# Pooled attention and a snake expert layer in f32: one more product of the hidden layer in the inner seven-product form, and the softmax one or two slots later

## The chip, the cores and the metric

One core of one Trainium2 chip runs the whole program. The metric is the device time of one execution in microseconds, as the median of several runs; before the change it is 899.29 us (three runs, 898.45 to 900.01). The profile is one execution of the same program with the hardware profiler on.

## The reference

Inputs q, k, v are f32 of shape (8, 8, 576, 64): batch, heads, sequence, head dimension. Keys and values are averaged over pools of 8 positions, so that each head has 72 keys. The result of the attention goes, head by head, into rows of 512 numbers and through two matrices with a snake activation in between:

```
k_p = k.reshape(B, H, 72, 8, D).mean(axis=3)          # v_p likewise
scores = scale * q @ k_p^T;  attn = softmax(scores)
x = (attn @ v_p) as (4608, 512)
h = x @ w_in                                          # 512 x 2048
s = sin(alpha * h)
g = h + s * s / (alpha + 1e-9)
out = g @ w_out                                       # 2048 x 512
```

All of it is in f32, and the output is (4608, 512).

## The kernel before

**Stages.** The first product (x @ w_in) runs in nine units of 512 rows, u = 0 to 8; the second (g @ w_out) follows in six units and takes the rest of the span. Between them g goes through a tensor in HBM (g_bridge). While unit u of the hidden layer runs, the attention of batch u+1 is worked out piece by piece beside it.

**The seven products.** Both matrix products use Winograd's form of Strassen's scheme: a product of 2x2 blocks is made of seven block products instead of eight, with sums of blocks before and after. In the hidden layer the outer scheme halves the rows (2 x 256), the 512 inputs (2 x 256) and the 2048 outputs (2 x 1024). The weights of product p are `self.A[p]`; the sums of x are `self.bt`. Each unit runs four groups J = 0 to 3 (`begin`, object `G`; `Q` is the group before), each with two blocks of 128 of the 1024 outputs in each half. Product p of a group is four matmuls of 128x128 weights on 256 columns (`product`, L866): two output blocks `jj`, two input blocks `kk`.

Some products of some groups are themselves made by the seven-product scheme (`inner_product`, L1058): instead of four matmuls of 256 columns, seven of 128 columns. Its steps are `a` (first and fifth inner product into the spare PSUM bank `y`, then two copies on ScalarE), `b` (sixth and second, one copy), `d` (seventh, one addition on VectorE, L1073) and `e` (third and fourth). The sums of weights come from `inner_w_in` (once, in unit 0, GpSimd), those of x from `inner_x` (in slot 2 of each unit, GpSimd, L823). Which groups do so stands in `I5` (outer product 5) and `I1` (outer product 1): in units 1 to 6 groups 2 and 3 for product 5, group 3 for product 1.

**Slots.** A group has seven slots, `k` = 0 to 6, one for each outer product in the order 1, 5, 6, 2, 7, 3, 4; slot = 7 J + k runs from 0 to 27. `hidden` writes down, slot by slot, what each engine does; engines run their own instructions strictly in that order and wait for each other by semaphores. The results of the seven products are combined in four PSUM banks of the group (`b1`, `b6`, `b5`, `b7`, out of five that rotate), by ScalarE copies (L839) from bank to bank onto which PE adds, and by VectorE additions (`add`, L838). Sines and squares are on ScalarE (`sin` L1028, `square` L1035); some of them belong to the group before and run a few slots late (`last_sines`, `squares`), as do the two additions that make g final (`finish`, L1080) and the stores to HBM (`store_g`, L1094).

**What is carried beside it.** `carry(u)` puts functions into slots (`at(slot, f)`; they run where `hidden` calls `extras()`, or ahead of the slot for halves such as 24.5). For batch u+1 in units 1 to 6: the scores in slots 3 and 5 (PE, L318) with their maxima and differences on VectorE (L341, L342); `exp` on ScalarE (L367; Exp is in another activation table than Sin, so that a table load stands before and after); `norm`: sum and reciprocal on VectorE (L373, L374), the quotient on GpSimd (L375); `turn`: 32x32 transposes of the attention on VectorE into the tile `tr` (L504 to L514); `move`: 16 DMAs on SyncE's queue that carry `tr` into `aM` (L524), each reading columns that all four `turn` write; `all_values` in slot 25: attention times values on PE (L613, L626), from `aM`. In slots 23 to 26 of units 0 to 5, `turn_q` (L229, L234, DMAs L244) transposes the queries of batch u+2; there is one tile `tr`, which it uses again. In the middle of it `finish_before` makes a part of `finish` that had been put off:

```
for e in range(2):
    x = main[:, 4 * e:4 * e + 4]...
    nc.vector.transpose(out=out, in_=x)
    if e == 0:
        self.finish_before()
```

That addition (L1080) reads bank `b7` of group 2, which `all_values` takes for its second set of products (`rest`). `load_k`, `load_v`, `pool_k`, `pool_v` bring the keys and values of coming batches (DMA on SyncE's queue) and sum them over pools (GpSimd, L132, L152).

Of the kernel before, what the change touches and what calls it, by code (L numbers as in the profile page):

```python
# [19 lines left out]
P = 128  # L20
# [20 lines left out]
class Kernel:  # L41
# [793 lines left out]
    def hidden(self, u, extra):  # L835
# [3 lines left out]
        copy = lambda o, x: nc.scalar.copy(out=o, in_=x)  # L839
        sin, square, early = self.sin, self.square, lambda G: G.J == (0 if G.u else 1)  # L840
        busy = 0 < u < self.B - 1
        I5, I1 = ((2, 3), (3,)) if busy else {7: ((2, 3), (2, 3)), 8: ((2, 3), (2, 3))}.get(u, ((), ()))
        split = lambda J: u == 0 and J == 2
        end = lambda J: u == 0 and J == 3

        def begin(J):
# [30 lines left out]
        for slot in range(7 * self.NJ):  # L877
            J, k = divmod(slot, 7)
            Q, G = self.before, self.group

            def extras():
                for f in extra[slot]:
                    f()
            for f in extra[slot - 0.5]:
                f()

            if k == 0:
                Q = self.before = G
                N = self.next
                G = self.group = N or begin(J)  # L890
                self.next = None
                if G.i5 and not N:
                    G.i5.a()
                if Q and not G.i5 and not end(J):
                    self.last_sines(Q, 2)
                extras()
                if G.i1:
                    G.i5.b()
                    self.last_sines(Q, 0)
                else:  # L900
                    product(G, 1, G.b1, True)
                    if G.i5:
                        product(Q, 4, Q.b7, part=(2, 3))
            elif k == 1:
                if not G.i1:
                    copy(G.b6[:], G.b1[:])
                if G.i5 and not G.i1:
                    self.last_sines(Q, 0)
                elif Q and not G.i1:
                    if end(J):  # L910
                        self.last_sines(Q, 2)
                    for i in (0,) if split(J) else (1, 0) if u == 0 else (0, 1):
                        squares(Q, i)
                extras()
                if not G.i5:
                    product(G, 5, G.b5, True)
            elif k == 2:
                if Q and not G.i5 and not split(J):
                    self.finish(Q)
                if not G.i1:  # L920
                    extras()
                if G.i1:
                    product(G, 6, G.b6, part=(0, 1))
                    G.i5.d()
                    self.last_sines(Q, 1)
                    square(Q, 1, 0)
                    self.late = Q
                    extras()
                    self.finish_before()
                    product(G, 6, G.b6, part=(2, 3))  # L930
                elif G.i5:
                    product(G, 6, G.b6, part=(0, 1))
                    G.i5.b()
                    self.last_sines(Q, 1)
                    squares(Q, 0)
                    product(G, 6, G.b6, part=(2, 3))
                else:
                    product(G, 6, G.b6)
            elif k == 3:
                late = J == 0 and busy  # L940
                if Q and not late and not G.i5 and not split(J):
                    self.store_g(Q)
                G.p5 = self.tp.tile([P, JW, TH], F32, name="p5")
                if G.i1:
                    if not busy:
                        copy(G.b7[:], G.b6[:])
                    square(Q, 1, 1)
                    squares(Q, 0)
                    extras()
                    product(G, 2, G.b1)  # L950
                    G.i5.e()
                    copy(G.p5[:], G.b5[:])
                else:
                    copy(G.b7[:], G.b6[:])
                    if G.i5:
                        squares(Q, 1)
                        G.i5.d()
                        self.finish(Q)
                        self.store_g(Q)
                    else:  # L960
                        copy(G.p5[:], G.b5[:])
                    if split(J):
                        squares(Q, 1)
                        self.finish(Q, (0,))
                    extras()
                    product(G, 2, G.b1)
            elif k == 4:
                if G.i1 and busy:
                    copy(G.b7[:], G.b6[:])
                    self.behind_order = lambda: sin(G, 0, 0, G.b1)  # L970
                else:
                    sin(G, 0, 0, G.b1)
                if not G.i5:
                    square(G, 0, 0)
                extras()
                if G.i1:
                    self.finish(Q, (1,))
                    self.store_g(Q)
                product(G, 7, G.b7, part=(0, 1))
                if G.i5:  # L980
                    if not G.i1:
                        G.i5.e()
                        copy(G.p5[:], G.b5[:])
                    square(G, 0, 0)
                product(G, 7, G.b7, part=(2, 3))
            elif k == 5:
                add(G.g[:, 1, :, 1], G.b7[:], G.p5[:])
                extras()
                if split(J):
                    self.finish(Q, (1,))  # L990
                    self.store_g(Q)
                N = None
                if J + 1 in I1:
                    N = self.next = begin(J + 1)
                    N.i1.a()
                product(G, 3, G.b6, part=(0, 1))
                if N:
                    N.i1.b()
                product(G, 3, G.b6, part=(2, 3))
            else:  # L1000
                if J == 0 and busy and Q:
                    self.store_g(Q)
                add(G.g[:, 0, :, 1], G.b6[:], G.p5[:])
                sin(G, 1, 1, G.g[:, 1, :, 1])
                N = self.next
                last = lambda: add(G.g[:, 0, :, 0], G.b1[:], G.s[:, 0, :, 0])
                if not N:
                    last()
                    extras()
                    product(G, 4, G.b7, part=(0, 1))  # L1010
                    if J + 1 not in I5 or J + 1 in I1:
                        product(G, 4, G.b7, part=(2, 3))
                else:
                    product(G, 4, G.b7, part=(0,))
                    N.i1.d()
                    last()
                    N.i5.a()
                    product(G, 4, G.b7, part=(1, 2))
                    N.i1.e()
                    copy(N.b6[:], N.b1[:])  # L1020
                    extras()
                    product(G, 4, G.b7, part=(3,))

    def sin(self, G, i, j, src):

        for jj in range(JW):
            f = i * self.K2 // 2 + G.J * JW + jj
            self.nc.scalar.activation(out=G.s[:, i, jj, j, :], in_=src[:, jj], func=AF.Sin, scale=self.al[:, f:f + 1])  # L1028
# [173 lines left out]
    def carry(self, u):  # L1202
# [6 lines left out]
        if u == 0:  # L1209
# [37 lines left out]
            at(19, A.move, (3,), nc.scalar)  # L1247
            at(26, A.all_values)
            at(9, self.load_q, 2)
            at(23, lambda: self.inner_w_in(((5, 2, 4), (1, 3, 4)), (lambda w: [w[:, i * 2 * P:i * 2 * P + 2 * P] for i in range(8)])(self.q_tile(0))))  # L1250
            for e in range(2):
                at(12, self.load_k, 2, e)
                at(17, lambda e=e: self.pool_k[e]())
# [5 lines left out]
        if 0 < u < last:  # L1259
            A = self.att[b]  # L1260
            for i in range(2):
                at((3, 5)[i], A.two_scores, i)
            at(6, A.two_shifts)
            for i in range(4):
                at((8, 9, 10, 10)[i], A.exp, i)
                at((9, 10, 11, 12)[i], A.norm, i)
                at((12, 13, 13, 13)[i], A.turn, i)
            at(14, A.move, range(4))
            at(6, self.load_v, b)
            at(12, lambda: self.pool_v())  # L1270
            for i in range(2):
                if b < last:
                    at(12, self.load_k, b + 1, i)
                    at(12, lambda i=i: self.pool_k[i]())
            at(25, A.all_values)
            if b < last:
                at(26, self.att[b + 1].k_t)
            if 2 < u + 2 <= last:
                at(7, self.load_q, u + 2)
            at(2, self.inner_x, u)  # L1280
            turn = 22
        elif u:
            turn = None
# [429 lines left out]
```

## Time and profile before

| | |
|---|---|
| median of three runs | 899.29 us (898.45 to 900.01) |
| span of the profiled execution | 896.2 us |
| hidden layer, units 0 to 8, L866 and L1058 | 19 to 513 us of the span |
| unit 2, as an example | 137 to 193 us, some 55 us each |
| L866 (256 columns) | 1808 matmul records |
| L1058 (128 columns) | 364 matmul records |
| out product, L1383 | 505 to 893 us |

How to read it. Every f32 matmul leaves two records, with two weight loads (PEld) beside them. A matmul's duration in the rows is longer than its step in the stream, since neighbours overlap; the distance from one start to the next is what it costs. A row of the timeline is: start in us from the span's beginning, length in us, engine, line, operation, out<-in, shapes, count, and in brackets the idle time of the engine before it with what ended it. Rows of one kind that follow each other are merged, and the length then runs from the first start to the last end. SPq are DMA issues on SyncE's queue; their length is the time of issuing, not of landing. In the tables by line the figures behind the bar are busy us, mean ns of one, and idle us before.

### The profile page before, as it was taken

How to read it: one execution, taken by the hardware profiler on the slowest of the kernel's cores; microseconds unless marked ns; L12 is line 12 of the kernel's file. 1: busy time of each engine (PE TensorE's matmuls, PEld its weight loads, DVE VectorE, ACT ScalarE, POOL GpSimd, SP SyncE). 2: the span in 40 equal slices, each digit the busy share in tenths (PEclk: the TensorE clock that was granted, in tenths of full speed). 3: DMA queues.
4: the chain of work that ended last, by engine and by line, in shares of the span. 5: the costliest groups of instructions: out<-in, count | busy, mean ns of one | idle time of the engine just before them, and what ended most of it. 6: DMA issues, size and time to landing. Idle time of an engine off the chain costs nothing.

```text
span 896.2 us, 16276 instructions
## 1 busy us (share of the span) xinstructions
PE 890.8 (99%) x6274; PEld 813.9 (91%) x6274; DVE 682.9 (76%) x918; ACT 438.6 (49%) x1033; POOL 249.2 (28%) x265
## 2 busy tenths in 40 slices
PE   9999999999999999999999999999999999999998
PEld 6787888888888888888888999999999999999998
DVE  7786857768577675765677889898897896996885
ACT  6687776877768777687776711111111211111111
POOL 6798443825338252434523000000000000000000
PEclk9999999999999999999999999999999999999999
DMA  9857957759586585648126243716435355164002
GB/s 269 244 158 206 244 147 212 187 164 254 139 214 186 183 225 147 175 140 302 53 106 219 102 181 103 232 37 218 117 105 160 89 159 159 37 192 142 20 18 53
DMA packets 119533, 141.03 MB, mean 157 GB/s; under 512 B 45776, under 2 KB 86496, under 8 KB 119456
## 3 DMA queue, kind: packets, MB, share of 16 engines
q1 hardware_dynamic: 116288, 137.39, 52.6%
q10 hardware_dynamic: 3168, 2.61, 1.0%
q8 instruction: 50, 0.82, 0.4%
q14 instruction: 27, 0.22, 0.1%
HBM read 75.37 MB, written 47.19 MB: 137 GB/s over the span
## 4 chain that ended last, share of the span: by engine, by line
PE 99%; DVE 0%; POOL 0%; ACT 0%; issue 0%; DVEq 0%
PE PS L866 44%; PE PS L1383 43%; PE PS L1058 5%; PE PS L318 2%; PE PS L613 2%; PE PS L626 1%; PE PS L1126 0%; PE PS L571 0%; PE PS L290 0%; PE PS L425 0%; PE PS L279 0%; PE PS L479 0%; PE PS L569 0%; POOL tr L451 0%; PE PS L403 0%; PE PS L487 0%
## 5 line engine op out<-in xcount | busy, mean ns | idle before, releaser
L866 PE MATMUL PS<-home,a 128*128 128x256 f32 x1072 | 253.0, 381 | 0.1
L866 PEld LDWEIGHTS PS<-home,a 128*128 128x128 f32 x1072 | 198.4, 190 | 30.9 <-issue 4.6
L866 PE MATMUL PS<-home,as 128*128 128x256 f32 x736 | 177.2, 382 | 0.0
L866 PEld LDWEIGHTS PS<-home,as 128*128 128x128 f32 x736 | 134.5, 190 | 18.1 <-ACT PS L839 1.2
L1383 PE MATMUL PS<-s,wb 128*128 128x192 f32 x672 | 116.2, 326 | 0.0
L1035 ACT ACTIVATE s<-s,c 128x256 f32<-128x256 f32 (+1 forms) x236 | 115.5, 556 | 0.0
L1383 PEld LDWEIGHTS PS<-s,wb 128*128 128x128 f32 x672 | 110.4, 190 | 0.1
L132 POOL TENSOR_TENSOR kvin<-kvin 96x768 f32<-96x768 f32 (+3 forms) x42 | 73.4, 1747 | 69.9 <-DMA kvin<-in_v_dram 67.8
L838 DVE TENSOR_TENSOR h<-PS,p 128x512 f32<-128x512 f32 x72 | 49.2, 684 | 55.5 <-PE PS L866 35.2
L1554 ACT COPY PS<-PS 128x192 f32<-128x192 f32 x42 | 12.7, 303 | 146.2 <-PE PS L1383 130.0
L1028 ACT ACTIVATE s<-h,al 128x256 f32<-128x256 f32 x144 | 65.5, 509 | 32.6 <-DVE h L838 32.6
L1383 PE MATMUL PS<-r,wb 128*128 128x192 f32 x432 | 79.0, 326 | 0.0
L1383 PEld LDWEIGHTS PS<-r,wb 128*128 128x128 f32 x432 | 71.6, 190 | 0.0
L1383 PE MATMUL PS<-s,a 128*128 128x192 f32 x384 | 70.2, 326 | 0.0
L1028 ACT ACTIVATE s<-PS,al 128x256 f32<-128x256 f32 x144 | 60.0, 469 | 17.2 <-PE PS L866 16.5
L1383 PEld LDWEIGHTS PS<-s,a 128*128 128x128 f32 x384 | 63.7, 190 | 0.0
L1080 DVE TENSOR_TENSOR h<-PS,s 128x512 f32<-128x512 f32 x36 | 24.8, 689 | 48.6 <-ACT s L1035 48.6
L839 ACT COPY PS<-PS 128x512 f32<-128x512 f32 x72 | 41.5, 577 | 34.5 <-PE PS L866 26.7
L1080 DVE TENSOR_TENSOR h<-h,s 128x1024 f32<-128x1024 f32 x36 | 55.3, 1537 | 3.3 <-ACT s L1035 3.1
L1584 ACT COPY PS<-PS 128x192 f32<-128x192 f32 x42 | 12.7, 303 | 89.5 <-PE PS L1383 89.5
L1322 DVE TENSOR_TENSOR s<-r 128x768 f32<-128x768 f32 x54 | 51.4, 951 | 4.8 <-PE PS L1383 2.8
L1383 PE MATMUL PS<-s,we 128*128 128x192 f32 x288 | 52.7, 326 | 0.0
(244 smaller groups left out, 1401.4 us busy)
## 6 DMA issues: line engine op xcount, KB each, us to landing
g_bridge<-h SPq DMA_DIRECT2D x72, 512.0 KB
r<-g_bridge SPq DMA_DIRECT2D x15, 1536.0 KB
x<-g_bridge SPq DMA_DIRECT2D x8, 1536.0 KB
out_dram<-o SPq DMA_DIRECT2D x90, 96.0 KB
kvin<-in_k_dram SPq DMA_DIRECT2D x14, 576.0 KB
q<-in_q_dram SPq DMA_DIRECT2D x7, 1024.0 KB
kvin<-in_v_dram SPq DMA_DIRECT2D x14, 512.0 KB
aM<-tr SPq DMA_DIRECT2D x54, 92.0 KB
```

What stands on the lines that cost most here:

```text
L132: self.nc.gpsimd.tensor_tensor(out=t[..., 0:w] if w > D else out, in0=t[..., 0:w], in1=t[..., w:2 * w], op=OP.add)
L318: nc.tensor.matmul(ps[e][r0 + r:r0 + r + q.shape[-1], h, :], q[s], kb[s, hp, :], start=True, stop=True)
L613: nc.tensor.matmul(o[r:r + 64], w, x, start=start and i < 2, stop=False, skip_group_check=True)
L838: add = lambda o, x, y: nc.vector.tensor_tensor(out=o, in0=x, in1=y, op=OP.add)
L839: copy = lambda o, x: nc.scalar.copy(out=o, in_=x)
L866: nc.tensor.matmul(ps[:, jj, :], self.A[p][:, kk, f * P:(f + 1) * P], x[:, kk, :], start=(start and n == 0), stop=(kk == 1), skip_group_ch ...
L1028: self.nc.scalar.activation(out=G.s[:, i, jj, j, :], in_=src[:, jj], func=AF.Sin, scale=self.al[:, f:f + 1])
L1035: self.nc.scalar.activation(out=x, in_=x, func=AF.Square, scale=self.c[:, f:f + 1])
L1058: nc.tensor.matmul(o, W[m][:, G.J - J0], X[m], start=start and n == 0, stop=True, skip_group_check=True)
L1080: add = lambda o, x, y: self.nc.vector.tensor_tensor(out=o, in0=x, in1=y, op=OP.add)
L1322: tt = lambda o, x, y, op: nc.vector.tensor_tensor(out=o, in0=x, in1=y, op=op)
L1383: nc.tensor.matmul(out, W[:, J // 2, J % 2, :], A[:, J, :], start=(start and J == 0), stop=(J == self.NJ - 1), skip_group_check=True)
```

## The change

In units 1 to 6, group 1 also makes its fifth product in the inner form: `I5` there goes from (2, 3) to (1, 2, 3), and the weight sums of product 5 are made for groups 1 to 3 instead of 2 and 3. `fast(G)` is true for that group, and its steps are placed by hand: `a` in slot 7, `b` in slot 8, `d` in slot 9, `e` in slot 10; half of the fourth product of group 0 goes from slot 6 to slot 8, some sines and squares are put to other slots, and `sin(G, 1, 1, ...)` of group 1 goes from slot 13 into slot 15. In `carry`, for units 1 to 6, `exp` goes from slots 8, 9, 10, 10 to 10, 10, 10.5, 10.5; `norm` from 9, 10, 11, 12 to 11, 11, 12, 13; `turn` from 12, 13, 13, 13 to 12, 13, 14, 14; `pool_v` and `pool_k` from 12 to 14. `move` stays in slot 14, `all_values` in 25, `turn_q` where it was.

```diff
-        I5, I1 = ((2, 3), (3,)) if busy else {7: ((2, 3), (2, 3)), 8: ((2, 3), (2, 3))}.get(u, ((), ()))
+        I5, I1 = ((1, 2, 3), (3,)) if busy else {7: ((2, 3), (2, 3)), 8: ((2, 3), (2, 3))}.get(u, ((), ()))
+        fast = lambda G: busy and G.J == 1
...
             if k == 0:
+                if fast(G):
+                    self.last_sines(Q, 0)
...
                     product(G, 1, G.b1, True)
-                    if G.i5:
+                    if G.i5 and not fast(G):
                         product(Q, 4, Q.b7, part=(2, 3))
             elif k == 1:
                 if not G.i1:
                     copy(G.b6[:], G.b1[:])
-                if G.i5 and not G.i1:
+                if fast(G):
+                    G.i5.b()
+                    product(Q, 4, Q.b7, part=(2, 3))
+                    self.last_sines(Q, 1)
+                    squares(Q, 1)
+                elif G.i5 and not G.i1:
+                    if fast(Q):
+                        sin(Q, 1, 1, Q.g[:, 1, :, 1])
                     self.last_sines(Q, 0)
...
             elif k == 2:
+                if fast(G):
+                    product(G, 6, G.b6, part=(0, 1))
+                    G.i5.d()
+                    self.finish(Q)
                 if not G.i1:
                     extras()
-                if G.i1:
+                if fast(G):
+                    product(G, 6, G.b6, part=(2, 3))
+                elif G.i1:
...
             elif k == 3:
-                    if G.i5:
+                    if fast(G):
+                        product(G, 2, G.b1, part=(0, 1))
+                        G.i5.e()
+                    elif G.i5:
...
                     extras()
-                    product(G, 2, G.b1)
+                    if fast(G):
+                        copy(G.p5[:], G.b5[:])
+                    product(G, 2, G.b1, part=(2, 3) if fast(G) else range(4))
             elif k == 4:
-                if not G.i5:
+                if not G.i5 or fast(G):
                     square(G, 0, 0)
                 extras()
...
-                if G.i5:
+                if G.i5 and not fast(G):
...
             else:
-                sin(G, 1, 1, G.g[:, 1, :, 1])
+                if not fast(G):
+                    sin(G, 1, 1, G.g[:, 1, :, 1])
...
-            at(23, lambda: self.inner_w_in(((5, 2, 4), (1, 3, 4)), (lambda w: [w[:, i * 2 * P:i * 2 * P + 2 * P] for i in range(8)])(self.q_tile(0))))
+            at(23, lambda: self.inner_w_in(((5, 1, 4), (1, 3, 4)), (lambda w: [w[:, i * 3 * P:i * 3 * P + 3 * P] for i in range(4)] + [w[:, 12 * P + i * P:13 * P + i * P] for i in range(4)])(self.q_tile(0))))
...
             for i in range(4):
-                at((8, 9, 10, 10)[i], A.exp, i)
-                at((9, 10, 11, 12)[i], A.norm, i)
-                at((12, 13, 13, 13)[i], A.turn, i)
+                at((10, 10, 10.5, 10.5)[i], A.exp, i)
+                at((11, 11, 12, 13)[i], A.norm, i)
+                at((12, 13, 14, 14)[i], A.turn, i)
             at(14, A.move, range(4))
             at(6, self.load_v, b)
-            at(12, lambda: self.pool_v())
+            at(14, lambda: self.pool_v())
             for i in range(2):
                 if b < last:
                     at(12, self.load_k, b + 1, i)
-                    at(12, lambda i=i: self.pool_k[i]())
+                    at(14, lambda i=i: self.pool_k[i]())
```

More of the change, by code (lines that the diff above doesn't have):

```diff
@@ L940, in hidden @@
                 late = J == 0 and busy
-                if Q and not late and not G.i5 and not split(J):
+                if Q and not late and (not G.i5 or fast(G)) and not split(J):
                     self.store_g(Q)
```

## The prediction

> **What bounds the kernel now.** I read the page first, then the waits, then unit 2 (137 to 193 us of the span) engine by engine in order of time.
>
> ```profile
> span 896.2 us, 16276 instructions
> PE 890.8 (99%) x6274; PEld 813.9 (91%) x6274; DVE 682.9 (76%) x918; ACT 438.6 (49%) x1033; POOL 249.2 (28%) x265
> PEclk9999999999999999999999999999999999999999
> PE 99%; DVE 0%; POOL 0%; ACT 0%; issue 0%; DVEq 0%
> ```
>
> PE is busy through the whole span at the full granted clock, and the chain that ended last is 99% PE. So the time is PE's own work plus every wait that PE is made to take; the other engines matter only where they make PE wait. The profiled execution spans 896.2 us, the median of the runs is 899.29, so 3.1 us lie around the span; I forecast on the span and add them back.
>
> **PE's work.** The rows below are the start of group 2 (J=2) of unit 2, which already has the seven-product form.
>
> ```profile
> 165.35 0.38 PE L1058 MATMUL PS<-home,as 128*128 128x128 f32 x2
> 165.79 2.76 PE L866 MATMUL PS<-home,a 128*128 128x256 f32 x12
> 168.39 1.09 PE L866 MATMUL PS<-home,as 128*128 128x256 f32 x4
> ```
>
> Each f32 matmul leaves two records. Two 128-column matmuls take 165.79-165.35 = 0.44 us; twelve records (six matmuls) of 256 columns take 168.39-165.79 = 2.60, or 0.433 each. The change takes four 256-column matmuls (1.73 us) out of group 1 in units 1 to 6 and puts in seven of 128 columns (7 x 0.22 = 1.54): 0.19 us less for each unit, 1.1 us in all. The wider sums of w_in are made once, on POOL in unit 0; one of before is
>
> ```profile
> 78.59 0.72 POOL L823 TENSOR_TENSOR q<-as,q 128x256 f32<-128x256 f32 x1
> ```
>
> and half as much again on four of them is about 1.4 us at 80 us of the span, long before group 1 of unit 1 (its moves start at 114.64, and group 1 some 16 us ahead of them, as 153.2 stands to 169.70 in unit 2 below). So I cost them at nothing; without that cover it would be 1.4 us, once.
>
> [...]
>
> **Where the other engines move.** With the fifth product in the new form, ACT gets three small copies more in group 1, and DVE one addition. The four exponentials go from slots 8 to 10 into slot 10 and the half slot after it, the quotients (DVE sum and reciprocal, POOL multiply) to slots 11, 11, 12, 13, the transposes (L504 to L514) to 12, 13, 14, 14. On DVE this gives the order: first two sums, first transpose, third sum, the two additions that close group 1 (L838), second transpose, fourth sum, third transpose, fourth transpose. Before, the fourth sum stood ahead of those last two additions. That matters, because the second of them waits for ACT's squares of s[0,0], and these now stand behind all exponentials and both table loads. The 16 moves of the transposed scores (L524, SP) wait for the end of the fourth transpose. I follow this chain through unit 2 with durations, or start-to-start distances, of before.
>
> ```profile
> 152.35 3.62 PE L866 MATMUL PS<-home,a 128*128 128x256 f32 x16
> 156.01 0.57 ACT L839 COPY PS<-PS 128x512 f32<-128x512 f32 x1 [0.30 <-PE PS L866]
> 156.49 1.33 ACT L1035 ACTIVATE s<-s,c 128x512 f32<-128x512 f32 x2
> 157.84 1.28 ACT L367 ACT_TABLE_LOAD   x1
> 159.13 1.26 ACT L367 ACTIVATE ex<-ex 128x576 f32<-128x576 f32 x2
> 160.30 0.58 ACT L839 COPY PS<-PS 128x512 f32<-128x512 f32 x1
> 161.29 1.49 ACT L367 ACTIVATE ex<-ex 128x576 f32<-128x576 f32 x2
> 162.80 1.28 ACT L1028 ACT_TABLE_LOAD   x1
> 164.10 0.84 ACT L1028 ACTIVATE s<-PS,al 128x256 f32<-128x256 f32 x2
> 164.82 0.90 ACT L1035 ACTIVATE s<-s,c 128x256 f32<-128x256 f32 x2
> ```
>
> PE begins the fourth product of group 0 at 152.35. After the change come half of it (0.87), the first inner pair (0.44), product 1 (1.73), the second inner pair (0.44) and the other half (0.87): 156.70. ACT has the result 0.20 later (PE passes to product 5 at 152.35+16 x 0.216 = 155.81, the copy starts at 156.01), so its sines of b7 start at 156.90. From there ACT runs without a gap: sines 0.72, squares 1.35, copy 0.48 (156.01 to 156.49), table load 1.29, two exponentials 1.17, copy 0.48, two exponentials 1.51, table load 1.30, sines 0.72, squares 0.90. That is 9.92, and the squares of s[0,0] end at 166.82, 1.1 us later than before (164.82+0.90 = 165.72).
>
> ```profile
> 164.39 1.02 DVE L373 TENSOR_REDUCE sm<-ex 128x12 f32<-128x876 f32 x1
> 165.44 0.23 DVE L374 RECIPROCAL sm<-sm 128x12 f32<-128x12 f32 x1
> 165.82 1.63 POOL L375 TENSOR_TENSOR ex<-ex,sm 128x864 f32<-128x864 f32 x1 [1.30 <-ACT s L1035]
> 166.13 0.68 DVE L838 TENSOR_TENSOR h<-PS,s 128x512 f32<-128x512 f32 x1
> 166.73 0.70 DVE L504 STREAM_TRANSPOSE tr<-ex 128x512 f32<-128x512 f32 x1
> 167.55 0.67 DVE L504 STREAM_TRANSPOSE tr<-ex 128x512 f32<-128x512 f32 x1
> 168.34 0.67 DVE L504 STREAM_TRANSPOSE tr<-ex 128x512 f32<-128x512 f32 x1
> 169.70 10.08 SPq L524 DMA_DIRECT2D aM<-tr  x16
> ```
>
> DVE's closing addition starts at 166.85 and takes 0.60; second transpose 0.82; fourth sum 1.05; from its reciprocal to POOL's multiply 0.38; the multiply 1.63: 171.33, with the third transpose beside it. Only then the fourth transpose, 1.36 from its start to the first move (168.34 to 169.70): 172.69. So **the moves start 3.0 us later than before**, in every one of the units 1 to 6.
>
> **Who waits for the moves.** SP issues them one behind the other, 10.08 us in unit 2, and nothing can hurry them. Two things stand behind the last one. PE's values (L613) read aM. And turn_q of the same unit (units 1 to 5) writes tr, the tile the moves read: its first transpose (L229) waits for all of them, and behind it on DVE stands the addition L1080 (finish_before), which frees the PSUM bank that PE's second group of value products writes.
>
> ```profile
> 65.52 7.88 SPq L524 DMA_DIRECT2D aM<-tr  x12
> 75.14 2.37 DVE L229 STREAM_TRANSPOSE tr<-q 128x1024 f32<-128x1024 f32 x2 [0.22 <-DMA aM<-tr]
> ...
> 114.64 11.20 SPq L524 DMA_DIRECT2D aM<-tr  x16
> 127.45 1.25 DVE L229 STREAM_TRANSPOSE tr<-q 128x1024 f32<-128x1024 f32 x1
> 128.62 0.65 DVE L1080 TENSOR_TENSOR h<-PS,s 128x512 f32<-128x512 f32 x1
> 129.85 0.65 PE L613 MATMUL PS<-aM,vm 64*64 64x512 f32 x6
> ```
>
> The first two rows are unit 0, where this wait already showed: L229 sat idle until the moves had landed, and started 1.74 us after SP was through with them (65.52+7.88 = 73.40). In unit 1 it started 1.61 us after SP's end (114.64+11.20 = 125.84), which bounds the landing from above there; I take 1.61. L1080 ends 1.82 us after L229's start, and PE can write 0.1 later. PE's second group stands 0.12 behind the first L613 row, at 129.97 in unit 1, where the addition frees the bank at 127.45+1.82+0.10 = 129.37. So before, 0.6 us were to spare in unit 1, and the moves now come 3.0 us late.
>
> ```profile
> 184.92 0.65 PE L613 MATMUL PS<-aM,vm 64*64 64x512 f32 x6
> 224.77 10.74 SPq L524 DMA_DIRECT2D aM<-tr  x16
> 239.98 0.65 PE L613 MATMUL PS<-aM,vm 64*64 64x512 f32 x6
> 280.17 10.08 SPq L524 DMA_DIRECT2D aM<-tr  x16
> 295.23 0.65 PE L613 MATMUL PS<-aM,vm 64*64 64x512 f32 x6
> 335.09 10.70 SPq L524 DMA_DIRECT2D aM<-tr  x16
> 350.30 0.65 PE L613 MATMUL PS<-aM,vm 64*64 64x512 f32 x6
> ```
>
> **The sum.** For each unit: end of SP's stretch + 3.0 + 1.61 + 1.82 + 0.10, against the first L613 row + 0.12.
> - unit 1: 125.84 + 6.53 = 132.37 against 129.97: +2.40
> - unit 2: 179.78 + 6.53 = 186.31 against 185.04: +1.27
> - unit 3: 235.51 + 6.53 = 242.04 against 240.10: +1.94
> - unit 4: 290.25 + 6.53 = 296.78 against 295.35: +1.43
> - unit 5: 345.79 + 6.53 = 352.32 against 350.42: +1.90
>
> Together +8.9. The shorter product is inside these figures (they compare ends, so PE just waits 0.19 longer). Unit 6 has no turn_q and keeps its gain, -0.2. Span 896.2+8.7 = 904.9, runs about **908.0 us**, 1.0% slower.
>
> Other terms stay near nothing. The copy of b6 after group 2's first product ends at about 168.15, PE wants it at 168.20; the addition inside the fifth product of group 2 stands behind the fourth transpose and comes just in time. Each can cost 0 to 0.2 us for a unit, but in units 1 to 5 what PE loses there it need not wait for later. POOL's sums of v and k are pushed back behind the last quotient, but only the values and the transposes of k after them want these. SP's next moves, those of q, start later too; the scores of the next unit want them, a whole stretch of moves later. Nothing excludes a small gain where a short wait of PE vanishes: I allow 0.3 us in all.
>
> **The rivals.**
> - *Only the gain* (not slower): no wait reaches PE, 899.29-1.1 = 898.2. It needs moves no more than about 0.4 us later than before in unit 1 (the 0.6 less PE's 0.19). For it: PE is the chain now. Against: the order on DVE, and L229 at its limit already.
> - *A shorter delay*: the squares finish early, or POOL's multiply hides. With the moves 2.0 us later each unit loses 1.0 less: 1.40+0.27+0.94+0.43+0.90-0.2 = 3.7, or 903.0.
> - *A longer tail*: the delay reaches 3.6 us, because instructions take longer beside new neighbours (no row shows that for these), 5 x 0.6 = 3.0 more: 911.
> - *The weight loads set the pace* for 128 columns:
>
> ```profile
> L1058 PEld LDWEIGHTS PS<-last,q 128*128 128x128 f32 x72 | 12.8, 191 | 1.2
> ```
>
>   at 0.19 us for each, one behind the other, fourteen of them are 2.7 us against 1.73, 5.6 us in all: 905 without any other wait. That two matmuls with their four loads go by in 0.44 us speaks against it: the loads overlap.
>
> **Chances.** The forecast 0.70, shorter delay 0.09, longer tail 0.08, only the gain 0.11, weight loads 0.02. What a measurement can tell from no change is about 0.2%, or 1.8 us: the gain alone is inside it. Faster by more than that needs gains that no row shows, 0.04 (out of the gain case); within it 0.08 (the other 0.07 of the gain case and 0.01 of the shorter delay); slower 0.88. The forecast's own range, with 0.4 us either way on the 3.0 (2 us over five units), is 905.5 to 910.5; to hold 8 in 10 I go from 903.0 to 911.0, which leaves out the gain case and half of the longer tail.
>
> **What would show it.** In the profile after: PE idle at the first L613 of units 1 to 5 with the moves or L1080 named; L229 idle until the moves landed, in all of them; moves first issued about 3 us later against group 2's first inner pair (4.35 us before: 165.35 to 169.70); group 1 shorter by 0.19 us. I am wrong if the fourth transpose ends within a microsecond of where it did, or if PE's rows show no gap ahead of L613.

## The result, and the profile after

The changed kernel takes 910.89 us (median of four runs, 909.31 to 911.99) against 899.65 us before (898.45 to 901.15) in the same series: the ratio is 1.0126, 95% interval 1.0113 to 1.0139. The forecast was 908.0, in a range of 903 to 911. The profiled run took 911.98 us, with a span of 910.2.

The page after: span, busy shares, and the chain of work that ended last by engine and by line.

```profile
span 910.2 us, 16372 instructions
PE 898.7 (99%) x6310; PEld 815.4 (90%) x6310; DVE 687.0 (75%) x924; ACT 442.3 (49%) x1051; POOL 249.4 (27%) x265
...
PE 89%; SPq 4%; ACT 2%; DVE 2%; DMA 1%; issue 1%; POOL 0%; DVEq 0%; ACTq 0%; POOLq 0%
PE PS L1405 42%; PE PS L867 36%; SPq L524 4%; PE PS L1080 3%; PE PS L318 2%; PE PS L613 2%; DMA aM<-tr 1%; ACT s L1057 1%; PE PS L626 1%; DVE h L1102 1%; DVE tr L229 1%; PE PS L1148 0%; ACT s L1050 0%; ACT PS L839 0%; DVE sm L445 0%
```

PE's busy share is 99% as before, so it doesn't show the loss; the chain does. Before, it was 99% PE. Now 4% of it are the moves' issues on SyncE (L524), followed by their landing, turn_q's transpose (L229) and the addition in finish_before. The changed kernel's lines are numbered a little differently: L866 is L867 now, and from L1028 on they stand 22 higher, so that L1035 is L1057, L1058 is L1080, and the addition L1080 is L1102. L229, L373, L504, L524, L613, L838 and L839 keep their numbers.

Unit 2 of the changed kernel in order of time (start, length, engine, line). The unit's first score matmul is at 147.48, against 144.15 before, so 3.33 us are to be taken off to stand beside the prediction's times. The row of before, and then the rows after:

```profile
144.15 1.33 PE L318 MATMUL PS<-kblk,q 64*64 64x72 f32 x64
```

```profile
147.48 0.54 PE L318 MATMUL PS<-kblk,q 64*64 64x72 f32 x15
168.91 2.76 PE L867 MATMUL PS<-home,a 128*128 128x256 f32 x12
169.25 0.90 ACT L1057 ACTIVATE s<-s,c 128x256 f32<-128x256 f32 x2
170.18 0.69 DVE L838 TENSOR_TENSOR h<-PS,s 128x512 f32<-128x512 f32 x1 [0.60 <-ACT s L1057]
170.96 0.57 ACT L839 COPY PS<-PS 128x512 f32<-128x512 f32 x1 [0.34 <-DVE h L838]
171.59 1.13 PE L867 MATMUL PS<-home,as 128*128 128x256 f32 x4
171.61 1.02 DVE L373 TENSOR_REDUCE sm<-ex 128x12 f32<-128x876 f32 x1
174.70 0.71 DVE L504 STREAM_TRANSPOSE tr<-ex 128x512 f32<-128x512 f32 x1 [1.05 <-POOL ex L375]
176.12 10.08 SPq L524 DMA_DIRECT2D aM<-tr  x16
188.12 1.25 DVE L229 STREAM_TRANSPOSE tr<-q 128x1024 f32<-128x1024 f32 x1 [2.46 <-DMA aM<-tr]
188.16 1.08 PE L613 MATMUL PS<-aM,vm 64*64 64x512 f32 x4
189.29 0.65 DVE L1102 TENSOR_TENSOR h<-PS,s 128x512 f32<-128x512 f32 x1
190.00 0.33 PE L613 MATMUL PS<-aM,vm 64*64 64x64 f32 x4 [0.76 <-DVE h L1102]
204.28 0.54 PE L318 MATMUL PS<-kblk,q 64*64 64x72 f32 x15
```

Read it downwards: the squares end at 170.15; the closing addition waited 0.60 us for them; only behind it come the fourth sum and, through POOL, the fourth transpose; the moves start at 176.12. At the other end L229 sat idle for 2.46 us until the moves had landed, the addition L1102 stands behind it, and PE waited for that addition. The row's 0.76 us is the smaller part of this wait, since the matmuls at 188.16 are drawn 1.08 us long: before, the second group of values began 0.12 behind the first, and here it begins 1.84 behind it (190.00 - 188.16). The 1.72 us between the two are what the unit lost (1.73, below). Counted from the unit's first score matmul, the moves start 28.64 us in (176.12 - 147.48), against 25.55 before (169.70 - 144.15): 3.09 us later.

The lengths of the units, from one first score matmul to the next, of the changed kernel's first profile and of a second one taken with the experiments:

| unit | before | after | more | forecast | second profile, more |
|---|---|---|---|---|---|
| 1 | 55.07 | 57.18 | 2.11 | 2.40 | 2.10 |
| 2 | 55.07 | 56.80 | 1.73 | 1.27 | 1.73 |
| 3 | 55.25 | 60.13 | 4.88 | 1.94 | 2.40 |
| 4 | 55.06 | 56.79 | 1.73 | 1.43 | 1.72 |
| 5 | 55.07 | 56.72 | 1.65 | 1.90 | 1.65 |

Unit 3 stands out in the first profile. From the timeline, its moves and the two rows in which PE waited:

```profile
232.92 11.79 SPq L524 DMA_DIRECT2D aM<-tr  x16
246.42 1.08 PE L613 MATMUL PS<-aM,vm 64*64 64x512 f32 x4 [1.38 <-DMA aM<-tr]
248.29 0.33 PE L613 MATMUL PS<-aM,vm 64*64 64x64 f32 x4 [0.79 <-DVE h L1102]
```

And the windows around them (window, its length, busy time and instructions of PE, PEld, DVE, ACT, POOL, granted clock, DMA share, GB/s):

```profile
244.00:249.00 5.00, 2.83 (x31) 1.68 (x33) 2.59 (x3) 2.15 (x5) 0.00 (x0) 1.00 0.79 265
249.00:253.00 4.00, 4.00 (x36) 1.54 (x28) 2.07 (x3) 0.90 (x3) 0.00 (x0) 0.57 0.28 66
253.00:257.00 4.00, 3.99 (x22) 2.98 (x19) 1.16 (x2) 3.57 (x12) 0.00 (x0) 1.00 0.53 127
```

The moves took SyncE 11.79 us there, 1.05 more than before in this unit, so PE waited twice, 1.38 and 0.79 us by the rows; behind that the mean granted clock of four microseconds was 0.57, which cost an estimated 4 x 0.43 = 1.7 us. Narrower windows show what the mean hides: the clock stood at 0.50 from 249.4 to 252.8, for 3.4 us, and at 1.0 on either side. In two of the four runs the mean clock was 0.998 (911.98 and 911.99 us), in the other two 1.0 (909.31 and 909.8).

### The profile page after: what moved, and what is told of

It reads as the page before. It is cut to its first block, busy times and chain, and to the rows that moved or that the text cites. A ratio compares the mean times of both kernels' runs of the same rounds, so it can differ in the third digit from the quotient of the medians.

```text
span 910.2 us, 16372 instructions
## 1 busy us (share of the span) xinstructions
PE 898.7 (99%) x6310; PEld 815.4 (90%) x6310; DVE 687.0 (75%) x924; ACT 442.3 (49%) x1051; POOL 249.4 (27%) x265
## 4 chain that ended last, share of the span: by engine, by line
PE 89%; SPq 4%; ACT 2%; DVE 2%; DMA 1%; issue 1%; POOL 0%; DVEq 0%; ACTq 0%; POOLq 0%
PE PS L1405 42%; PE PS L867 36%; SPq L524 4%; PE PS L1080 3%; PE PS L318 2%; PE PS L613 2%; DMA aM<-tr 1%; ACT s L1057 1%; PE PS L626 1%; DVE h L1102 1%; DVE tr L229 1%; PE PS L1148 0%; ACT s L1050 0%; ACT PS L839 0%; DVE sm L445 0%
## 5 line engine op out<-in xcount | busy, mean ns | idle before, releaser
L867 PE MATMUL PS<-home,a 128*128 128x256 f32 x1072 | 255.9, 381 | 0.1
L867 PEld LDWEIGHTS PS<-home,a 128*128 128x128 f32 x1072 | 197.5, 190 | 29.8 <-issue 4.9
L867 PE MATMUL PS<-home,as 128*128 128x256 f32 x688 | 168.1, 383 | 0.0
L867 PEld LDWEIGHTS PS<-home,as 128*128 128x128 f32 x688 | 125.0, 190 | 17.1 <-ACT PS L839 1.8
L1057 ACT ACTIVATE s<-s,c 128x256 f32<-128x256 f32 (+1 forms) x236 | 115.5, 556 | 0.0
L132 POOL TENSOR_TENSOR kvin<-kvin 96x768 f32<-96x768 f32 (+3 forms) x42 | 71.2, 1695 | 69.8 <-DMA kvin<-in_v_dram 68.1
L838 DVE TENSOR_TENSOR h<-PS,p 128x512 f32<-128x512 f32 x72 | 49.4, 686 | 53.5 <-PE PS L867 34.4
L1102 DVE TENSOR_TENSOR h<-h,s 128x1024 f32<-128x1024 f32 x36 | 55.9, 1552 | 3.3 <-ACT s L1057 3.1
L839 ACT COPY PS<-PS 128x512 f32<-128x512 f32 x72 | 41.7, 579 | 30.5 <-PE PS L867 20.9
L1405 PEld LDWEIGHTS PS<-s,we 128*128 128x128 f32 x288 | 47.8, 190 | 0.1
```

The source lines that it names most:

```text
L132: self.nc.gpsimd.tensor_tensor(out=t[..., 0:w] if w > D else out, in0=t[..., 0:w], in1=t[..., w:2 * w], op=OP.add)
L838: add = lambda o, x, y: nc.vector.tensor_tensor(out=o, in0=x, in1=y, op=OP.add)
L867: nc.tensor.matmul(ps[:, jj, :], self.A[p][:, kk, f * P:(f + 1) * P], x[:, kk, :], start=(start and n == 0), stop=(kk == 1), skip_group_ch ...
L1057: self.nc.scalar.activation(out=x, in_=x, func=AF.Square, scale=self.c[:, f:f + 1])
L1102: add = lambda o, x, y: self.nc.vector.tensor_tensor(out=o, in0=x, in1=y, op=OP.add)
L1405: nc.tensor.matmul(out, W[:, J // 2, J % 2, :], A[:, J, :], start=(start and J == 0), stop=(J == self.NJ - 1), skip_group_check=True)
```

## The experiments

**The two halves of the change, each alone.** First the later slots without the new product:

```diff
 (before)
-                at((8, 9, 10, 10)[i], A.exp, i)
-                at((9, 10, 11, 12)[i], A.norm, i)
-                at((12, 13, 13, 13)[i], A.turn, i)
+                at((10, 10, 10.5, 10.5)[i], A.exp, i)
+                at((11, 11, 12, 13)[i], A.norm, i)
+                at((12, 13, 14, 14)[i], A.turn, i)
...
-            at(12, lambda: self.pool_v())
+            at(14, lambda: self.pool_v())
...
```

> The kernel before with the later slots alone: exponentials, quotients, transposes and the sums of v and k where the changed kernel has them, the fifth product of group 1 in its old form (16 matmuls of 256 columns). Theory (the late fourth transpose makes the loss, whatever the product's form): the squares of s[0,0] stand behind the four exponentials again, end about 1.5 us later than before, the fourth sum behind the closing additions; the moves start 3.0 to 3.6 us later than before, PE waits ahead of L613 in units 1 to 5 as in the changed kernel, and the gain of 0.19 us a unit is missing. Beside it the copy of b6 that PE's second product of group 2 wants comes later, up to 0.9 us a unit. 899.6 + 11 to 12.5 = 911 to 912. Rival (the inner form itself is what costs, through its small copies and additions, and the later slots are hidden): no wait ahead of L613, 899.6 as before.

Measured: 914.37 us, ratio 1.017 (1.0155 to 1.0186). The later slots alone lose all that the change loses, and more. From the views of one line, what L613 waited for (idle us of its engine, times, over the whole run):

```profile
  DVE h L1080: 3.0, 5
  DMA aM<-tr: 0.9, 1
```

and L866:

```profile
  DVE h L838: 3.2, 6
```

The waits are those of the changed kernel, at the same place, and beside them the one for the copy of b6, once in each of the units 1 to 6. The time passed the expected 912 by 2.4 us: the moves start 3.75 us later than before against the unit's start (177.71 in unit 2, which begins at 148.41), a little more than the 3.0 to 3.6 expected, and SyncE took 11.71 us for them in unit 3. The rival, that the inner form itself costs, is out as the cause of these waits.

Then the new product with the old slots:

```diff
 (after)
-                at((10, 10, 10.5, 10.5)[i], A.exp, i)
-                at((11, 11, 12, 13)[i], A.norm, i)
-                at((12, 13, 14, 14)[i], A.turn, i)
+                at((8, 9, 10, 10)[i], A.exp, i)
+                at((9, 10, 11, 12)[i], A.norm, i)
+                at((12, 13, 13, 13)[i], A.turn, i)
...
-            at(14, lambda: self.pool_v())
+            at(12, lambda: self.pool_v())
...
```

> The changed kernel with the slots of before for the exponentials, quotients, transposes and sums of v and k; the fifth product of group 1 in the inner form. Theory: moves start no more than about 0.8 us later against the unit's start than before, so no wait ahead of L613; but two exponentials now stand ahead of the copy of b7 on ACT, and PE waits about 1.2 us a unit for that copy at the seventh product of group 1: 899.6 - 1.1 + 6 x 1.2 = about 905.5, with PE's wait inside group 1 and not at L613. Rival 1 (the form brings only its gain): 898.5. Rival 2 (the inner form itself makes the late moves): waits at L613 as in the changed kernel, about 911.

Measured: 905.92 us, ratio 1.0074 (1.0059 to 1.0089). L613 waited for nothing in units 1 to 6; L867 waited for ScalarE, and unit 2 shows where:

```profile
161.36 1.28 ACT L367 ACT_TABLE_LOAD   x1
162.65 1.26 ACT L367 ACTIVATE ex<-ex 128x576 f32<-128x576 f32 x2
163.82 0.58 ACT L839 COPY PS<-PS 128x512 f32<-128x512 f32 x1
164.45 1.35 PE L867 MATMUL PS<-home,a 128*128 128x256 f32 x5 [1.08 <-ACT PS L839]
173.28 10.07 SPq L524 DMA_DIRECT2D aM<-tr  x16
```

The copy of b7 stands behind a table load and two exponentials, and PE's seventh product waits for it. So the old slots do not suit the new product: with them it costs 1.2 us a unit at another place. The moves start 1.2 us late here (26.75 us into the unit, where at most 0.8 was expected), but PE comes 1.1 us later to its values too (41.90 against 40.77 us into the unit), and nobody waits for them.

**Where the delay comes from.** The changed kernel with the fourth quotient back ahead of the closing additions:

```diff
 (after)
-                at((11, 11, 12, 13)[i], A.norm, i)
-                at((12, 13, 14, 14)[i], A.turn, i)
+                at((11, 11, 12, 12)[i], A.norm, i)
+                at((13, 13, 14, 14)[i], A.turn, i)
```

> The changed kernel with the fourth quotient one slot earlier (slots 11, 11, 12, 12; transposes 13, 13, 14, 14), so that the fourth sum stands ahead of the closing additions of group 1 on DVE, as before the change; everything else as in the changed kernel. Theory (the closing addition, late through ACT's squares, ahead of the fourth sum is what makes the moves 3.0 us late): the moves start about 1.6 us later than before instead of 3.1, PE's waits ahead of L613 shrink to about 1.0 in unit 1, 0.6 in units 3 and 5, 0.1 in unit 4: 901.2 (900.5 to 903). Rival (the later exponentials alone make the moves late, the order on DVE does not matter): moves 3 us late as before, 910.9.

Measured: 900.83 us, ratio 1.0024 (1.0014 to 1.0034). Unit 2 in its timeline:

```profile
166.47 1.02 DVE L373 TENSOR_REDUCE sm<-ex 128x12 f32<-128x876 f32 x1
168.50 0.69 DVE L838 TENSOR_TENSOR h<-PS,s 128x512 f32<-128x512 f32 x1 [0.20 <-ACT s L1057]
171.50 0.67 DVE L504 STREAM_TRANSPOSE tr<-ex 128x512 f32<-128x512 f32 x1
172.87 10.07 SPq L524 DMA_DIRECT2D aM<-tr  x16
```

The sum stands 2.0 us ahead of the closing addition instead of 1.4 behind it, the moves start 1.53 us late instead of 3.09, and four fifths of the loss are gone (0.0024 of 0.0126). The exponentials are as late as in the changed kernel, so their lateness alone doesn't make it. The reverse, the same reordering in the kernel before:

```diff
 (before)
-                at((9, 10, 11, 12)[i], A.norm, i)
-                at((12, 13, 13, 13)[i], A.turn, i)
+                at((9, 10, 11, 13)[i], A.norm, i)
+                at((12, 13, 14, 14)[i], A.turn, i)
...
-            at(12, lambda: self.pool_v())
+            at(14, lambda: self.pool_v())
...
```

> The kernel before with the fourth quotient alone one slot later (slots 9, 10, 11, 13; transposes 12, 13, 14, 14; the sums of v and k at slot 14): no inner form in group 1, exponentials in their old slots. The fourth sum stands behind the closing additions of group 1. Theory: the moves start about 2.4 us later than before and PE waits ahead of or inside L613 by 1.8 in unit 1, 0.7 in unit 2, 1.3 in unit 3, 0.8 in unit 4, 1.3 in unit 5: 898.6 + 5.9 = 904.5 (903 to 906.5). Rival (only later exponentials make the wait, by way of ACT): 898.6.

Measured: 903.4 us, ratio 1.0058 (1.0043 to 1.0073). In unit 2, which begins at 145.67:

```profile
173.21 10.08 SPq L524 DMA_DIRECT2D aM<-tr  x16
```

The moves start 1.99 us late, 0.4 less than expected, and the time is 1.1 below the forecast. This reordering, with neither the new product nor a later exponential, costs 4.9 us. It also carries the sums of v and k from slot 12 to 14; these stand at 14 in the run with the earlier quotient too, where four fifths of the loss are gone, so they aren't what costs.

**How the delay reaches PE.** The changed kernel with finish_before called first:

```diff
 (after, turn_q)
-                nc.vector.transpose(out=out, in_=x)
                 if e == 0:
                     self.finish_before()
+                nc.vector.transpose(out=out, in_=x)
```

> The changed kernel with finish_before called ahead of the first transpose of turn_q, so that the addition that frees PE's bank no longer stands behind a transpose that waits for the moves. Theory (the wait runs moves, then turn_q's transpose, then that addition, then PE): PE waits only for the moves' own landing. From the landings in the changed kernel that is about 0.9 us in unit 1, 0.5 in unit 3, 0.4 in unit 5 and near 0 else; with the gain of 1.1 and small stalls at the sixth product of group 2 the sum is 901 (900 to 903). Rival (PE waits for the moves themselves, the addition is beside the point): 910.9, no change.

Measured: 901.38 us, ratio 1.0026 (1.0017 to 1.0036). Unit 2, and unit 3, where the moves are slowest to issue; the transpose is L231 here:

```profile
174.56 10.08 SPq L524 DMA_DIRECT2D aM<-tr  x16
185.21 0.69 DVE L1102 TENSOR_TENSOR h<-PS,s 128x512 f32<-128x512 f32 x1 [1.11 <-ACT s L1057]
186.56 2.37 DVE L231 STREAM_TRANSPOSE tr<-q 128x1024 f32<-128x1024 f32 x2 [0.66 <-DMA aM<-tr]
186.60 0.65 PE L613 MATMUL PS<-aM,vm 64*64 64x512 f32 x6
...
229.58 11.35 SPq L524 DMA_DIRECT2D aM<-tr  x16
```

The moves start 28.64 us into the unit, exactly as late as in the changed kernel, yet four fifths of the loss are gone here too (0.0026 of 0.0126 is left). The transpose still waits for the landing, but the addition is done before it, and PE goes on. What is left are waits for the landing itself, ahead of the first values: 0.92 us in unit 1 and 1.10 in unit 3, as the distance from one matmul's start to the next beyond the usual step of 0.22. So the wait ran through the addition behind the transpose.

**Both repairs.** The two diffs above together.

> The changed kernel with both repairs: the fourth quotient one slot earlier (slots 11, 11, 12, 12; transposes 13, 13, 14, 14) and finish_before called ahead of turn_q's first transpose. Theory: the moves start 1.5 us later than before, land about 1 us ahead of PE in every unit, and nothing on DVE that PE wants stands behind them; no wait ahead of or inside L613 is left. Of the inner form's gain of 1.1 us the stall at the sixth product of group 2 (about 0.1 us a unit more than before) takes 0.5: 898.0 against 898.6 of the kernel before, between 897.3 and 898.8. Rival (the two repairs take away the same wait, so that the second adds nothing): 900.8 as with the earlier quotient alone.

Measured: 898.78 us, ratio 1.0003 (0.9991 to 1.0014): no difference from before can be told. The chain of its page is PE's again:

```profile
PE 97%; DMA 2%; SPq 0%; issue 0%; POOL 0%; DVE 0%; POOLq 0%
```

and the timeline of unit 2 shows where the gain of the new product went:

```profile
146.60 0.60 PE L318 MATMUL PS<-kblk,q 64*64 64x72 f32 x19
167.59 0.38 PE L1080 MATMUL PS<-home,as 128*128 128x128 f32 x2
168.03 2.76 PE L867 MATMUL PS<-home,a 128*128 128x256 f32 x12
171.67 0.38 PE L1080 MATMUL PS<-last,q 128*128 128x128 f32 x2
```

Group 2 begins 20.99 us into the unit (167.59 - 146.60) against 21.20 before (165.35 - 144.15): the gain of about 0.2 us is real. But from the twelve records of 256 columns to the next inner pair it takes 171.67 - 168.03 = 3.64 us, where the kernel before took 169.31 - 165.79 = 3.52, up to this row:

```profile
169.31 0.39 PE L1058 MATMUL PS<-last,q 128*128 128x128 f32 x2
```

PE waits there for the copy of b6, which waits for the closing addition, which waits for the squares. Of 0.21 us a unit 0.12 are given back at once, and unit 4 of this profile lost another 0.3 (55.38 us long against 55.06), for a cause that wasn't followed. The repairs took away different waits, so the second did add something; but there was little left to win.

**What a longer wait does to the clock.** The changed kernel once more, and a dose:

> The changed kernel once more, for its unit 3, which lost 4.9 us in the first profile where the other units lost about 1.7 to 2.1. Theory (unit 3's moves take SP 0.7 to 1.7 us longer than those of units 2 and 4 every time, so PE waits longer there, and after that wait the granted clock falls for some us): unit 3 again loses 3 us or more, with the clock under 0.7 behind the first L613. Rival (the clock fell by chance): unit 3 loses about 2.5 us, with the clock at 1.0, and the span is 1.5 to 2 us shorter. The median stays at 910.9 either way within 1.5.

Measured: 911.69 us, ratio 1.0147 (1.0129 to 1.0164). The profiled execution had no fall: unit 3 is 57.65 us long, 2.4 more than before, at a clock of 1.0, with moves of 10.96 us; its span is 907.2. The other three runs had mean clocks of 0.998, 0.998 and 0.995, at 911.66, 911.73 and 914.02 us; the profiled one, at 1.0, 908.97. So the fall isn't bound to unit 3 of every run. That it comes by chance isn't shown by this: PE's waits at the values of unit 3 were shorter here, 0.56 and 0.79 us instead of 1.38 and 0.79, since the moves took less long.

```diff
 (after)
-                at((12, 13, 14, 14)[i], A.turn, i)
-            at(14, A.move, range(4))
+                at((12, 13, 14, 18)[i], A.turn, i)
+            at(18, A.move, range(4))
...
-            at(14, lambda: self.pool_v())
+            at(18, lambda: self.pool_v())
...
```

> The changed kernel with the fourth transpose, the moves and the sums of v and k at slot 18 in place of 14, behind three additions of DVE (L1095 and both L1102 of group 2's fifth product), which end at 179.76 in unit 2 of the changed kernel's profile. A dose, to see what a longer wait of PE does to the granted clock, which fell to 0.57 for about 4 us behind the 2 us of waits in unit 3 of the changed kernel, and stayed at 1.0 behind the waits of 0.7 to 1.4 us of the other units. The transposes run from 179.8, the moves start at 181.2 in place of 176.1, 5.1 us later, and PE waits as much longer in units 1 to 6: 911 + 6 x 5.1 = 941.5 (936 to 944) by the waits alone, mean clock 1.0 or 0.999. Theory (a wait of 2 us or more lowers the clock behind it each time): a stretch at 0.5 to 0.7 behind L613 in each of the six units, 4 x 0.43 = 1.7 us more for each, about 951, mean clock near 0.99. Rival (the falls come by chance, not with the wait): none or one such stretch, 941 to 944.

Measured: 954.04 us, ratio 1.0617 (1.0592 to 1.0642), mean clock 0.977 to 0.98. PE's wait in unit 2, from the timeline:

```profile
187.88 10.68 SPq L524 DMA_DIRECT2D aM<-tr  x16
200.26 2.44 PE L613 MATMUL PS<-aM,vm 64*64 64x512 f32 x8 [3.96 <-DMA aM<-tr]
```

and windows of 6 us around the first values of units 2, 3 and 6 (the clock is the third figure from the end):

```profile
200.00:206.00 6.00, 5.74 (x48) 2.72 (x48) 4.66 (x5) 0.90 (x3) 0.00 (x0) 0.50 0.14 32
265.00:271.00 6.00, 5.59 (x48) 2.72 (x48) 4.66 (x5) 0.90 (x3) 0.00 (x0) 0.50 0.13 31
458.00:464.00 6.00, 5.74 (x58) 3.84 (x59) 0.00 (x0) 1.23 (x5) 0.00 (x0) 0.72 0.43 161
```

The waits ahead of the first values are 4.88, 3.96, 4.80, 4.18, 3.95 and 4.61 us in units 1 to 6, and the clock fell at every one of them. Narrower windows give the length: in units 1 to 5 the clock stood at 0.50 for 6.8 us (199.5 to 206.4 in unit 2, so that it fell while PE still waited), in unit 6 for 3.4 us. The moves start 5.03 to 5.05 us later than in the changed kernel in units 1 to 5 and 3.96 in unit 6, which by the waits gives 911 + 25.2 + 4.0 = 940. Another 14 us came on top. SyncE's stretches are 3.7 us of that: the six took 10.68 to 11.54 us here, and 10.07 to 10.96 in the second profile of the changed kernel. The rest is 1.6 to 2.2 us for each unit. In unit 2 the values from their first L613 row on vz to L626 took 4.07 us (202.49 to 206.56), all but 0.16 of it at a clock of 0.50, against 2.16 in unit 2 of the changed kernel (190.16 to 192.32) at 1.0: 1.91 us more. The theory is nearer than the rival, with a longer fall than the 4 us that it put in. Between the 2.2 us of unit 3 in the first profile and the 3.95 us here no trace has a wait.

## Why the forecast held, and what it mis-sized

- **The delay of the moves** (3.0 us forecast) was 3.09. Less the 3.33 us by which unit 2 lies later, the squares end at 166.82 (forecast 166.82), the closing addition starts at 166.85 (166.85), the fourth sum at 168.28 (168.27) and the moves at 172.79 (172.69). This step held link by link, and putting the sum back ahead of the addition took half of the delay and four fifths of the loss away.
- **The way to PE** (landing, L229, L1102, bank) held: taking L1102 out from behind L229 gave back four fifths of the loss with the moves as late as ever. The prediction looked for PE's gap at the first L613 of each unit; in units 2, 4 and 5 it stands between the first values and the second, whose bank the addition frees.
- **The landing** was set at 1.61 us behind SyncE's end, from one row. It took 1.92 in unit 2 (186.20 to 188.12), and 1.61 to 1.85 in the other units. With the 0.09 on the start this makes 0.40 of the 0.46 by which unit 2 was over its forecast.
- **SyncE's stretches** were taken unit by unit from before's profile, as if they were a unit's own. They vary from run to run: unit 3's was 11.79, 10.96 in the second profile, 10.74 before; unit 1's 10.77 against 11.20 before, unit 5's 10.07 against 10.70. That explains why units 1 and 5 came out below the forecast, and 1.05 us of unit 3.
- **Unit 3** was forecast at +1.94 and came to +4.88: 1.05 from the stretch, 1.7 from the clock's fall, which the forecast had no term for, the rest from start and landing.
- **Unit 6**, forecast at -0.2, lost some 0.5: its first L613 stands 41.22 us into the unit (419.14 - 377.92) against 40.77. The unit has no turn_q. SyncE was through with the moves at 417.37, and PE began 1.77 us behind that, a landing's time, after an idle 0.48:

```profile
406.59 10.78 SPq L524 DMA_DIRECT2D aM<-tr  x16
419.14 0.65 PE L613 MATMUL PS<-aM,vm 64*64 64x512 f32 x6 [0.48 <-issue]
```

  The forecast looked for the wait behind L229 alone and overlooked that the landing by itself comes too late where the stretch is long.
- **The gain** (0.19 us a unit) was right: 0.21 in the run with both repairs. The copy of b6, allowed 0 to 0.2, took 0.12.
- **What lies around the span** (3.1 us) mixed two executions: in the runs after, time less span is 1.8 us (911.98 - 910.2). The rest was the distance of that profile from the median.

The forecast's loss was 8.7 us, the measured one 11.2. The median lies halfway between two runs at a mean clock of 1.0 and two at 0.998, which are 2.2 to 2.7 us longer. The two at 1.0 lost 9.9 us on average (909.56 - 899.65), so some 1.3 of the 2.5 us that were missed are the fall of the clock. The rest is of the size of unit 6, 0.7 over its forecast, and of units 1 to 5, which lost 9.6 us in the second profile, where the clock did not fall, against 8.9 forecast. What stands ahead of unit 1 is no part of the change: its first score matmul is at 90.30 and 89.82 in the two profiles against 89.08 before, but at 90.18 in the run with the later slots alone, whose unit 0 is that of before.

So the mechanism was forecast, link by link, and the size came out too small. That 910.89 lies inside the range, by 0.1 us, is partly luck: the same kernel's second series has a median of 911.69, above the range, and its run without a fall of the clock took 908.97.

Of the rivals, a longer tail (911) gave nearly the time, but not by its mechanism: the delay was 3.09, not 3.6. A shorter delay is out by the same number. Only the gain is out, as PE waits at L613 in every unit. The weight loads as pace are out, since group 1 became 0.21 us shorter.

Time against delay, for the runs in which the addition stands behind L229: 1.53 us gives 900.8, 1.99 gives 903.4, 3.09 gives 910.9, 3.75 gives 914.4. The first reach only the units with the least to spare. The second and the last are without the new product, and SyncE's stretches differ, so this is no clean curve; the cleanest pair is unit 2 of the last two, where SyncE took 10.08 us in both: 0.66 us of delay (28.64 to 29.30 into the unit) made it 0.67 longer (56.80 to 57.47).

## What to carry to other kernels

Where an engine runs its own instructions strictly in order, as VectorE does in these traces, a step moved by one slot takes on every wait that now stands ahead of it (here the fourth sum, 1.02 us long, took on an addition that waited 0.60 us for the squares): look at what the new neighbour waits for, not at what the step costs. A wait that touches the engine that bounds the kernel through a third engine's queue can be cut there, by calling what doesn't depend on the wait first; that gave back as much as halving the delay (901.38 us against 900.83). And a gain of 0.2 us in one stage was worth little here, because the next stage's inputs were not early by as much: with both repairs 0.12 of 0.21 us went at the next wait.

## What the runs showed of the hardware

In the profile of the kernel before, PE's granted clock was 1.0 from its first matmul to its last. In the profiles of the changed kernel and of the run with the moves in slot 18 it fell at some of PE's waits, stood at 0.50 for 3.4 us or for 6.8 us and was 1.0 again: for 3.4 us behind waits of 1.38 and 0.79 us in unit 3 of the changed kernel, and behind the wait of 4.61 us in unit 6 of the run with the moves in slot 18; for 6.8 us at each wait of 3.95 to 4.88 us in units 1 to 5 there. In the run with the later slots alone PE waited 0.95 and 0.79 us in unit 3, 1.7 us together, and the clock stayed at 1.0 (the window begins inside the first wait and takes in 1.4 us of the two):

```profile
248.00:252.00 4.00, 2.60 (x38) 1.24 (x42) 3.40 (x4) 1.57 (x5) 0.00 (x0) 1.00 0.70 262
```

In the first profile of the changed kernel PE was idle for 2.2 us between 244 and 249, in two pieces, and the clock fell. In these traces, then, waits of up to 1.7 us together left the clock at 1.0, 2.2 us saw it fall once, and 3.95 us or more every time, in six of six. Whether 2.2 us does so each time was not tried: four of the eight runs of the changed kernel have a mean clock of 0.998, which by an estimate from its size (1.7 of 910 us) is one fall of 3.4 us, one has 0.995 and three have 1.0, but only two of the eight have a trace.
